# Attention plus feed-forward on one core: the first two rows' QKV interleaved by weight slice

## The chip, the cores and the metric

The kernel runs on one core of one Trainium2 chip. The metric is the device time of one execution in microseconds, as a median over runs. Below, PE is TensorE, DVE is VectorE, ACT is ScalarE, POOL is GpSimd and SP is SyncE, which here only issues DMAs.

## The reference

One transformer block on x of shape (1, 2048, 576), bf16, with no weights in the layer norm:

```python
xn = _layernorm(x, axis=-1)
return x + _A_ref(xn, A_wqkv, A_wo) + _B_ref(xn, B_w_gate, B_w_up, B_w_down)
```

`_A_ref` is attention with 32 heads of 18: `qkv = xn @ wqkv` (576 to 1728), each position attends to 8 positions, itself and those 2, 4, ... 14 before it, with a softmax over the 8 logits, and the result goes through `wo`. `_B_ref` is `(silu(xn @ w_gate) * (xn @ w_up)) @ w_down` with 4608 hidden columns.

## The kernel before

**Tiling.** The 2048 positions are 16 "rows" of 128: position 16p + r lies in partition p of row r. Four rows make a token tile of 512. A row of x is normalised on DVE (two `bn_stats` of 288 columns, one `bn_aggr`, a square root on ACT, a reciprocal, `ln_apply` and a small pad copy), and turned, so that the 576 columns lie in partitions, in five blocks `kt` of 128 (the last holds the 64 remaining columns twice): `xnT[:, kt, row]`.

**Turning a row.** There are three ways. `transp_pe` makes five 128x128 matmuls against the identity. `transp_halves` makes ten 64-row matmuls into two PSUM banks, of which ACT empties one and DVE the other. `transp_dma` issues a DMA transpose on SP. Before, rows 0 and 1 take the first way, rows 2 to 4 the second (inside the QKV of the row before) and rows 5 to 15 the third.

**QKV (L267).** A row needs four column groups `g` of 432 columns, each in a PSUM bank of its own, accumulated over the blocks `kt`. The weights come as five slices, one for each `kt` (`load_w`; the fifth as two DMAs). Row 0 (`p_row0`) uses 128-row matmuls, 4 x 4, then four 64-row ones for the fifth block. The other rows (`p_row`) use 36 64-row matmuls, two at a time in the two halves of the array, first groups 0 and 2, then 1 and 3, and then the same with the halves swapped; the callback `between` puts the next row's turning after 24 of the 36.

**Evacuation.** `p_evac` copies a row's four banks on ACT: Q to `QO`, K and V to staging tiles. After rows 4, 8, 12 and 15, `halo` moves four staged rows to the K and V rings, one partition further on, and `store` writes whole groups to DRAM.

**Order.** The program is written out by hand: each engine runs its instructions in the order of the source, and waits where a tile isn't ready. All PSUM tiles come from one pool of 8 banks, taken in rotation; a bank is written again when its last tile has been emptied. Nearly all DMAs are issued on SP, in source order; row 0's second half and the first weight slice are issued on ACT. Before the first real work, `warm_pe` runs matmuls on zeros.

**After QKV.** For each token tile, nine chunks of the gate and up matmuls (`g_pair`, L522) with SiLU on ACT (`g_evac`), and then the down projection and `wo` (`d_half`, L551). DVE runs the attention meanwhile: `chain(tt)` queues its pieces, and `dve.take` and `dve.pump` emit them at fixed places of the source. The chain of the first tile starts during QKV, since its keys come through the rings. This part is not touched.

Of the kernel before, what the change touches and what calls it, by code (L numbers as in the profile page):

```python
# [17 lines left out]
P = 128  # L18
# [52 lines left out]
def kernel(  # L71
# [70 lines left out]
    def load_x(eng, j, rows=slice(0, P)):  # L142
        eng.dma_start(xc_b[0][rows, j, :], x_v[rows, j, :])  # L143

    def load_w(eng, kt):
        if kt < 4:
            eng.dma_start(wqkv[:, kt, :], A_wqkv[kt * P:(kt + 1) * P, :])  # L147
        else:
            for i in range(2):
                eng.dma_start(wqkvr[64 * i:64 * i + 64, :], A_wqkv[4 * P:D, 2 * G * i:2 * G * (i + 1)])  # L150

    load_x(nc.sync, 0, slice(0, 64))
    load_x(nc.scalar, 0, slice(64, 128))
    load_w(nc.scalar, 0)
    make_identity(nc, ident[:])
    load_w(nc.sync, 1)
    load_x(nc.sync, 1)
    for kt in range(2, KT):
        load_w(nc.sync, kt)
    load_x(nc.sync, 2)  # L160
    load_x(nc.sync, 3)
    for c in range(1, 4):
        nc.sync.dma_start(xc_b[c], x_v[:, 4 * c:4 * c + 4, :])
# [4 lines left out]
    def warm_pe(n):  # L168
        for i in range(n):
            nc.tensor.matmul(wp[:], wz[:, 0:P], wz[:, 0:512], start=True, stop=True)  # L170
# [18 lines left out]
    def new_ps(name):  # L189
        return ps.tile([P, 512], f32, name=name, tag="ps")  # L190
# [4 lines left out]
    def ln_open(c):  # L195
        mv = lns.tile([P, 4, 2], f32, name="mv")
        rstd = lns.tile([P, 4], f32, name="rstd")
        ln[c] = (xc_b[c], xn_b[c % 2], mv, rstd)

    def ln_stats(r, n=1):  # L200
        c, j = divmod(r, 4)
        xc, xn, mv, rstd = ln[c]
        for i in range(j, j + n):
            stats = lns.tile([P, 2, 6], f32, name="stats")
            for k in range(2):
                nc.vector.bn_stats(stats[:, k, :], xc[:, i, k * HALF:(k + 1) * HALF])  # L206
            nc.vector.bn_aggr(mv[:, i, :], stats[:].rearrange("p c s -> p (c s)"))

    def ln_sqrt(r, n=1):
        c, j = divmod(r, 4)  # L210
        xc, xn, mv, rstd = ln[c]
        nc.scalar.activation(rstd[:, j:j + n], mv[:, j:j + n, 1], ACT.Sqrt, bias=eps_t[:], scale=1.0)  # L212

    def ln_recip(r, n=1):
        c, j = divmod(r, 4)
        rstd = ln[c][3]
        nc.vector.reciprocal(rstd[:, j:j + n], rstd[:, j:j + n])
# [9 lines left out]
    def transp_pe(r, kts, pt):  # L227
        c, j = divmod(r, 4)
        xn = ln[c][1]
        for i, kt in enumerate(kts):  # L230
            nc.tensor.transpose(pt[:, i * P:(i + 1) * P], xn[:, j, kt * P:(kt + 1) * P], ident[:])

    def copy_pt(eng, r, kts, pt):
        eng(xnT[:, kts[0]:kts[-1] + 1, r * P:(r + 1) * P],
            pt[:, 0:len(kts) * P].rearrange("p (k t) -> p k t", t=P))
# [4 lines left out]
    def transp_halves(r):  # L240


        c, j = divmod(r, 4)
        xn = ln[c][1]
        pt = [new_ps("pt") for half in range(2)]
        for kt in range(KT):
            for half in range(2):
                rows = slice(64 * half, 64 * half + 64)
                nc.tensor.matmul(pt[half][:, kt * 64:(kt + 1) * 64], xn[rows, j, kt * P:(kt + 1) * P],
                                 ident[rows, rows], start=True, stop=True)  # L250
        for half, eng in enumerate((nc.scalar.copy, nc.vector.tensor_copy)):
            lo = r * P + 64 * half
            eng(xnT[:, :, lo:lo + 64], pt[half][:, 0:KT * 64].rearrange("p (k t) -> p k t", t=64))
# [11 lines left out]
    def p_mm(t, g, kt, half, r, start, stop):  # L265
        rows = slice(0, P) if half is None else slice(64 * half, 64 * half + 64)
        return nc.tensor.matmul(t[g][:, 0:G], xnT[rows, kt, r * P:(r + 1) * P], w_at(g, kt, rows),  # L267
                                start=start, stop=stop)

    def p_row0(between):  # L270
        t = [new_ps("qkv_ps") for g in range(NG)]
        for kt in range(4):
            for g in range(NG):
                p_mm(t, g, kt, None, 0, kt == 0, False)
            if kt == 2:
                between()
        for i in range(2):
            for half in range(2):
                p_mm(t, i + 2 * half, 4, half, 0, False, True)
        return t  # L280

    def fence_after(mm):
        f = nc.gpsimd.engine_nop()
# [6 lines left out]
    def p_row(r, between=None):  # L290


        t = [None] * NG
        fence = {}
        for swap in range(2):
            for i in range(2):
                kts = (0, 1, 2, 3) if swap else (0, 4, 1, 2, 3)
                for kt in kts:
                    for half in range(2):
                        g = i + 2 * (half ^ swap)  # L300
                        if t[g] is None:
                            t[g] = new_ps("qkv_ps")
                        mm = p_mm(t, g, kt, half, r, swap == 0 and kt == 0, swap == 1 and kt == 3)
                        if swap == 0 and kt == 3 and half == 1:
                            fence[i] = fence_after(mm)
                        if swap and kt == 0 and half == 0:
                            fence_before(mm, fence[i])
                    if swap and i == 0 and kt == 1 and between is not None:
                        between()
        return t  # L310

    def p_evac(r, t, between=None):
        c, j = divmod(r, 4)
        ks, vs = stage[2 * c % 4], stage[(2 * c + 1) % 4]
        vdst = vs[:, j, :].rearrange("p (d h) -> p d h", h=H)

        def v_copy(lo, n, src):
            nc.scalar.copy(vdst[:, :, lo:lo + n], src.rearrange("p (h d) -> p d h", d=DH))  # L318

        nc.scalar.copy(QO[:, r, 0:G], t[0][:, 0:G])  # L320
        if between is not None:
            between()
        nc.scalar.copy(ks[:, j, HALF:D], t[2][:, 0:HALF])
        v_copy(0, 8, t[2][:, HALF:G])
        nc.scalar.copy(QO[:, r, G:D], t[1][:, 0:D - G])
        nc.scalar.copy(ks[:, j, 0:HALF], t[1][:, D - G:G])
        v_copy(8, 24, t[3][:, 0:G])

    def halo(m, c):
        ring = Kr if m == 1 else Vr  # L330
# [85 lines left out]
        dve.add(0.3, done)  # L416


    def pair_stats(r):
        if r % 4 == 0:  # L420
            ln_open(r // 4)
        ln_stats(r, 2)
        ln_sqrt(r, 2)

    def pair_apply(r):
        ln_recip(r, 2)
        for i in (r, r + 1):
            ln_apply(i)
            if i > 4:
                transp_dma(i)  # L430

    def first():
        pt = new_pt()
        transp_pe(1, range(KT), pt)
        copy_pt(nc.scalar.copy, 1, range(3), pt)
        copy_pt(nc.vector.tensor_copy, 1, range(3, KT), pt[:, 3 * P:])
        ln_stats(2)

    warm_pe(10)
    ln_open(0)  # L440
    ln_stats(0)
    ln_sqrt(0)
    ln_recip(0)
    ln_apply(0, 0, P)
    pa, pb = new_pt(), new_pt()
# [1 line left out]
    ln_apply(0, P, D)  # L447
    transp_pe(0, range(1, KT), pb)
    copy_pt(nc.scalar.copy, 0, (0,), pa)
    warm_pe(1)  # L450
    copy_pt(nc.scalar.copy, 0, (1, 2), pb)
    ln_stats(1)
    copy_pt(nc.vector.tensor_copy, 0, (3, 4), pb[:, 2 * P:])
    ln_sqrt(1)
    ln_recip(1)
    ln_apply(1)
    for r in range(R):
        if r == 0:
            t = p_row0(first)
        else:  # L460
            t = p_row(r, (lambda: transp_halves(r + 1)) if r <= 3 else None)
        if r == 1:
            ln_recip(3)
            ln_apply(3)
        if r == 0:
            p_evac(r, t, lambda: ln_sqrt(2))
            ln_recip(2)
            ln_apply(2)
            ln_stats(3)
            ln_sqrt(3)  # L470
        else:
            p_evac(r, t)
        if 2 <= r <= 7:
            pair_apply(2 * r)
        if 1 <= r <= 6:
            pair_stats(2 * r + 2)
        if r == 0:
            load_gu(0)
            load_wd(7)
        if r == 1:  # L480
            for ring in (Kr, Vr):
                nc.sync.dma_start(ring[0:1, 0:HALO, :], wz[0:1, :].unsqueeze(1).to_broadcast([1, HALO, D]))
        if r == 2:
            load_wd(8)
        if r in (4, 8, 12, R - 1):
            c = (r - 1) // 4 if r < R - 1 else 3
            for m in (1, 2):
                halo(m, c)
                if c in (1, 2):
                    store(m, c)  # L490
            if c == 3:
                store(1, c)
        if r == 9:
            load_gu(1)
        if r == 7:
            chain(0)
        if r in (7, 8, 12):
            dve.take(3 if r == 7 else 6)


    wo_order = list(range(DH))
# [134 lines left out]
```

## Time and profile before

| What | Value |
|---|---|
| median of 3 runs | 505.94 us (505.89 to 506.33) |
| the profiled execution's own time | 506.33 us |
| its span | 504.5 us |
| granted TensorE clock | 1.0 |
| PE busy | 498.9 us, 99% of the span |
| DVE busy | 327.6 us, 65% |
| ACT busy | 200.2 us, 40% |
| QKV matmuls (L267) | 560, 53.8 us busy |
| gate and up matmuls (L522) | 2592, 281.4 us busy |
| down and output matmuls (L551) | 2304 + 288, 152.1 + 28.6 us busy |

Times in the profile count from the start of the span. A timeline row gives an instruction's start and length, its engine and line, what it writes and reads, how many were merged into it, and in brackets the idle time ahead of it with what ended it. A matmul's length is longer than its distance to the next one, since matmuls are pipelined. PE's share of busy time counts matmuls that lie beside each other once.

### The profile page before, as it was taken

The page shows a single profiled execution, that of the slowest core. Times are in us where ns is not written, and L with a number is a line of the kernel's source. Part 1 is how long each engine was busy: PE and PEld are TensorE (multiplying, and loading weights), DVE is VectorE, ACT ScalarE, POOL GpSimd, SP SyncE. Part 2 cuts the span into 40 slices and gives each one's busy share as a digit, 9 for nine tenths or more (in the row PEclk, how much of TensorE's full clock was granted, in tenths as well). Part 3 has the DMA queues.
Part 4 walks back from the last instruction along what each step waited for, and adds up shares of the span by engine and source line. Part 5 has one row for each costly group of instructions (what it writes and reads, how often), then busy time and mean ns, then how long its engine had stood idle before and what let it go on. Part 6 is the DMA issues. An engine that isn't in the chain of part 4 may idle for free.

```text
span 504.5 us, 13260 instructions
## 1 busy us (share of the span) xinstructions
PE 498.9 (99%) x5799; PEld 349.4 (69%) x5799; DVE 327.6 (65%) x475; ACT 200.2 (40%) x416; POOL 0.7 (0%) x6
## 2 busy tenths in 40 slices
PE   8999999999999999999999999999999999999997
PEld 3555544555799855555999755556999555557997
DVE  4985699798999688999898129995990222221001
ACT  2766566655400164555300354558000454553000
POOL 0000000000000000000000000000000000000000
PEclk9999999999999999999999999999999999999999
DMA  8998988878932037546631053555600236452100
GB/s 274 275 216 197 323 266 261 261 226 265 250 108 61 25 97 220 155 142 196 141 118 48 26 187 114 169 172 161 145 25 14 90 114 186 141 189 40 27 14 25
DMA packets 75811, 75.26 MB, mean 149 GB/s; under 512 B 21972, under 2 KB 71536, under 8 KB 75752
## 3 DMA queue, kind: packets, MB, share of 16 engines
q1 hardware_dynamic: 75384, 73.82, 50.8%
q8 instruction: 45, 0.74, 0.6%
q10 hardware_dynamic: 368, 0.59, 0.4%
q14 instruction: 14, 0.11, 0.1%
HBM read 58.76 MB, written 5.90 MB: 128 GB/s over the span
## 4 chain that ended last, share of the span: by engine, by line
PE 95%; ACT 2%; DMA 1%; SPq 1%; DVE 1%; issue 1%; ACTq 0%
PE g_ps L522 54%; PE d_ps L551 31%; PE qkv_ps L267 9%; DMA wd<-in_A_x_dram 1%; ACT uc L534 1%; SPq L147 0%; DVE stats L206 0%; ACT L533 0%; ACT L392 0%; SPq L150 0%; ACT sg L533 0%; SPq L143 0%; ACT rstd L212 0%; ACT PP L392 0%; DVE wd L222 0%
## 5 line engine op out<-in xcount | busy, mean ns | idle before, releaser
L522 PE MATMUL g_ps<-xnT,gu 64*128 64x512 bf16 x2592 | 281.4, 376 | 0.0
L522 PEld LDWEIGHTS <-gu 64*128 64x128 bf16 x2592 | 160.0, 94 | 120.0 <-DMA gu<-in_B_w_up_dram 0.5
L551 PE MATMUL d_ps<-wd,hT 64*128 64x288 bf16 x2304 | 152.1, 283 | 0.0
L533 ACT ACTIVATE sg<-g_ps 128x512 bf16<-128x512 f32 x144 | 87.3, 606 | 157.2 <-PE g_ps L522 157.1
L551 PEld LDWEIGHTS <-hT 64*128 64x128 bf16 x2304 | 144.3, 94 | 0.5
L535 DVE TENSOR_TENSOR hT<-sg,uc 128x512 bf16<-128x512 bf16 x144 | 60.1, 419 | 93.8 <-ACT uc L534 93.8
L534 ACT CAST uc<-g_ps 128x512 bf16<-128x512 f32 x144 | 85.2, 592 | 0.0
L372 DVE TENSOR_REDUCE PP<-PP 128x64 f32<-128x1152 bf16 x64 | 84.9, 1346 | 0.4
L267 PE MATMUL qkv_ps<-hT,xnT 64*128 64x432 bf16 (+1 forms) x560 | 53.8, 343 | 0.8 <-DMA hT<-in_A_wqkv_dram 0.6
L367 DVE TENSOR_TENSOR PP<-QO,Kr 128x2304 bf16<-128x2304 bf16 (+1 forms) x35 | 43.5, 1250 | 11.0 <-DMA Kr<-hT 10.7
L563 DVE TENSOR_TENSOR ot<-d_ps,xr 128x288 bf16<-128x288 f32 x30 | 12.3, 451 | 51.0 <-PE d_ps L551 51.0
L267 PEld LDWEIGHTS <-xnT 64*128 64x128 bf16 (+1 forms) x560 | 27.7, 94 | 25.5 <-issue 1.4
L399 DVE TENSOR_TENSOR PP<-Vr,A 128x2304 bf16<-128x2304 bf16 (+1 forms) x35 | 43.3, 1250 | 0.4
L404 DVE TENSOR_TENSOR PP<-PP 128x2304 bf16<-128x2304 bf16 x24 | 32.5, 1354 | 0.3
L551 PE MATMUL d_ps<-wo,xnT 64*128 64x288 bf16 x288 | 28.6, 283 | 0.0
L533 ACT ACT_TABLE_LOAD x5 | 6.4, 1283 | 47.2 <-PE g_ps L522 47.2
L551 PEld LDWEIGHTS <-xnT 64*128 64x128 bf16 x288 | 20.8, 94 | 0.0
L392 ACT ACTIVATE PP<-PP 128x1024 f32<-128x1024 f32 x4 | 4.2, 1057 | 31.2 <-DVE PP L388 31.2
L566 ACT CAST ot<-d_ps 128x288 bf16<-128x288 f32 x1 | 0.4, 399 | 38.7 <-PE d_ps L551 38.7
L206 DVE BATCH_NORM_STATS2 stats<-wd 128x6 f32<-128x288 bf16 x32 | 12.7, 440 | 3.7 <-DMA wd<-in_A_x_dram 3.6
L318 ACT CAST hT<-qkv_ps 128x144 bf16<-128x144 f32 (+1 forms) x32 | 13.9, 435 | 2.5 <-DMA kv_d<-hT 2.5
L320 ACT CAST QO<-qkv_ps 128x432 bf16<-128x432 f32 x16 | 8.3, 518 | 8.4 <-PE qkv_ps L267 8.4
(40 smaller groups left out, 98.0 us busy)
## 6 DMA issues: line engine op xcount, KB each, us to landing
gu<-in_B_w_gate_dram SPq DMA_DIRECT2D x36, 512.0 KB, 4.0
gu<-in_B_w_up_dram SPq DMA_DIRECT2D x36, 512.0 KB, 5.4
wd<-in_B_w_down_dram SPq DMA_DIRECT2D x9, 576.0 KB, 5.9
kv_d<-hT SPq DMA_DIRECT2D x6, 576.0 KB, 5.4
gu<-in_B_w_gate_dram SPq DMA_DIRECT2D x36, 64.0 KB, 5.0
gu<-in_B_w_up_dram SPq DMA_DIRECT2D x36, 64.0 KB, 4.7
xr<-in_A_x_dram SPq DMA_DIRECT2D x4, 576.0 KB, 5.5
out_dram<-ot SPq DMA_DIRECT2D x15, 144.0 KB, 1.8
```

The source lines that it names most:

```text
L206: nc.vector.bn_stats(stats[:, k, :], xc[:, i, k * HALF:(k + 1) * HALF])
L267: return nc.tensor.matmul(t[g][:, 0:G], xnT[rows, kt, r * P:(r + 1) * P], w_at(g, kt, rows), start=start, stop=stop)
L318: nc.scalar.copy(vdst[:, :, lo:lo + n], src.rearrange("p (h d) -> p d h", d=DH))
L367: nc.vector.tensor_tensor(prod[:, a:b], QO[:, RT * tt + a:RT * tt + b, :], Kr[:, s:s + b - a, :], op=ALU.mult)
L372: nc.vector.tensor_reduce(L[:, w, rs], prod[:, rs].rearrange("p r (h d) -> p r h d", d=DH), axis=AX.X, op=ALU.add)
L399: nc.vector.tensor_tensor(dst[:, a:b], Vr[:, s:s + b - a, :].rearrange("p r (d h) -> p r d h", h=H), A[:, w, a:b].unsqueeze(2).to_broadcas ...
L404: nc.vector.tensor_tensor(dst, acc, pv, op=ALU.add)
L522: mm = nc.tensor.matmul(ring_ps[j][b][:], gu[rows, slot, k, fc], xnT[rows, kt, tok], start=(swap == 0 and kt == 0), stop=(swap == 1 and kt ...
L533: nc.scalar.activation(sg[:], t[0][:], ACT.Silu)
L534: nc.scalar.copy(uc[:], t[1][:])
L535: nc.vector.tensor_tensor(hT[:, ch * FC + j, :], sg[:], uc[:], op=ALU.mult)
L551: mm = nc.tensor.matmul(t[sub][h][:, 0:HALF], a[rows], w[rows, h * HALF:(h + 1) * HALF], start=(swap == 0 and n == 0), stop=(swap == 1 and ...
```

## The change

- x rows 0 and 1 are loaded first, each half on SP's queue and half on ACT's. All weight slices are then issued on SP; x row 2 goes ahead of the fourth slice (before: behind the fifth).
- Rows 0 and 1 share the stage: row 0's blocks 0 and 1, the turning of row 1, row 0's block 2, row 1's blocks 0 to 2 for groups 0, 2 and 1, row 0's block 3 and last block, row 1's block 3 and last block for groups 0 and 2, the turning of row 2 (by `transp_pe`), and row 1's group 3. Row 1 uses 128-row matmuls as row 0 does. Three of row 1's banks are open beside row 0's four.
- Row 0's groups 2 and 3 are emptied by DVE, not ACT. The warm-up matmul between row 0's transposes and its QKV is gone.
- DVE's work is in another order: half of row 1's statistics lies between row 0's square root and reciprocal. The statistics of rows 4 and 5 follow row 3's copy in row 2 (before: in row 1), and their square root is inside row 2's evacuation.
- Rows 5 and 6 are turned by TensorE too, within the rows before them. Rows 7 to 15 stay with the DMA. Row 7's transpose is issued after the halos of rows 0 to 3, those of rows 14 and 15 after the halos of rows 4 to 7.
- The first nine attention pieces are emitted after row 8 (before: three after row 7, six after row 8).

```diff
-    load_x(nc.sync, 0, slice(0, 64))
-    load_x(nc.scalar, 0, slice(64, 128))
-    load_w(nc.scalar, 0)
+    for j in range(2):
+        load_x(nc.sync, j, slice(0, 64))
+        load_x(nc.scalar, j, slice(64, 128))
     make_identity(nc, ident[:])
-    load_w(nc.sync, 1)
-    load_x(nc.sync, 1)
-    for kt in range(2, KT):
+    for kt in range(3):
         load_w(nc.sync, kt)
     load_x(nc.sync, 2)
+    for kt in range(3, KT):
+        load_w(nc.sync, kt)
     load_x(nc.sync, 3)
...
-    def p_row0(between):
...
+    def p_full(t, r, kts, gs):
+        for kt in kts:
+            for g in gs:
+                p_mm(t, g, kt, None, r, kt == 0, False)
+
+    def p_pair(t, r, i):
+        for half in range(2):
+            p_mm(t, i + 2 * half, 4, half, r, False, True)
...
-    def p_evac(r, t, between=None):
+    def p_evac(r, t, parts=(0, 2, 1, 3), copy=None, between=None):
...
+        for g in parts:
+            if g == 0:
+                copy(QO[:, r, 0:G], t[0][:, 0:G])
+            elif g == 2:
+                copy(ks[:, j, HALF:D], t[2][:, 0:HALF])
+                v_copy(0, 8, t[2][:, HALF:G])
+                if between is not None:
+                    between()
+            elif g == 1:
+                copy(QO[:, r, G:D], t[1][:, 0:D - G])
+                copy(ks[:, j, 0:HALF], t[1][:, D - G:G])
+            else:
+                v_copy(8, 24, t[3][:, 0:G])
...
+    def pair_apply(r, by_pe):
         ln_recip(r, 2)
         for i in (r, r + 1):
             ln_apply(i)
-            if i > 4:
+            if i > by_pe:
                 transp_dma(i)
...
+    def turn(r, na):
         pt = new_pt()
-        transp_pe(1, range(KT), pt)
-        copy_pt(nc.scalar.copy, 1, range(3), pt)
-        copy_pt(nc.vector.tensor_copy, 1, range(3, KT), pt[:, 3 * P:])
-        ln_stats(2)
+        transp_pe(r, range(KT), pt)
+        copy_pt(nc.scalar.copy, r, range(na), pt)
+        copy_pt(nc.vector.tensor_copy, r, range(na, KT), pt[:, na * P:])
...
     ln_sqrt(0)
+    half1 = ln_half(1, None, 0)
     ln_recip(0)
...
-    warm_pe(1)
     copy_pt(nc.scalar.copy, 0, (1, 2), pb)
-    ln_stats(1)
+    ln_half(1, half1, 1)
...
+    t0 = {g: new_ps("qkv_ps") for g in (0, 2, 1, 3)}
+    p_full(t0, 0, range(2), t0)
+    turn(1, 3)
+    p_full(t0, 0, (2,), t0)
+    t1 = {g: new_ps("qkv_ps") for g in (0, 2, 1)}
+    p_full(t1, 1, range(3), (0, 2, 1))
+    p_full(t0, 0, (3,), t0)
+    for i in range(2):
+        p_pair(t0, 0, i)
+    ln_stats(2)
+    ln_sqrt(2)
+    ln_recip(2)
+    ln_apply(2)
+    p_evac(0, t0, (0, 1))
+    p_evac(0, t0, (2, 3), nc.vector.tensor_copy)
+    p_full(t1, 1, (3,), (0, 2, 1))
+    p_pair(t1, 1, 0)
+    turn(2, 3)
+    t1[3] = new_ps("qkv_ps")
+    p_full(t1, 1, range(4), (3,))
+    p_pair(t1, 1, 1)
+    ln_stats(3)
+    load_gu(0)
+    load_wd(7)
...
+    p_evac(1, t1, between=lambda: ln_sqrt(3))
+    ln_recip(3)
+    ln_apply(3)
+
+    BY_PE = 6
+    for r in range(2, R):
+        t = p_row(r, (lambda: transp_halves(r + 1)) if r < BY_PE else None)
+        if r == 2:
+            ln_stats(4, 2)
+            p_evac(r, t, between=lambda: ln_sqrt(4, 2))
+            pair_apply(4, BY_PE)
+            load_wd(8)
+        elif r == 3:
+            p_evac(r, t)
+            ln_stats(6, 2)
+            ln_sqrt(6, 2)
+        elif r == 5:
+            ln_stats(9)
+            p_evac(r, t, between=lambda: ln_sqrt(8, 2))
+            pair_apply(8, BY_PE)
+            ln_stats(10, 2)
+            ln_sqrt(10, 2)
         else:
             p_evac(r, t)
...
         if r in (4, 8, 12, R - 1):
             c = (r - 1) // 4 if r < R - 1 else 3
             for m in (1, 2):
                 halo(m, c)
...
+        if r == 4:
+            pair_apply(6, BY_PE)
+            ln_stats(8)
+        if r in (6, 7):
+            pair_apply(2 * r - 2, BY_PE)
+            ln_stats(2 * r, 2)
+            ln_sqrt(2 * r, 2)
+        if r == 8:
+            pair_apply(14, BY_PE)
         if r == 9:
             load_gu(1)
-        if r == 7:
+        if r == 8:
             chain(0)
-        if r in (7, 8, 12):
-            dve.take(3 if r == 7 else 6)
+        if r in (8, 12):
+            dve.take(9 if r == 8 else 6)
```

More of the change, by code (lines that the diff above doesn't have):

```diff
@@ L200, in ln_stats, with ln_half @@
     def ln_stats(r, n=1):
+        for i in range(r, r + n):
+            stats = ln_half(i, None, 0)
+            ln_half(i, stats, 1)
+    def ln_half(r, stats, k):
         c, j = divmod(r, 4)
         xc, xn, mv, rstd = ln[c]
-        for i in range(j, j + n):
+        if k == 0:
             stats = lns.tile([P, 2, 6], f32, name="stats")
-            for k in range(2):
-                nc.vector.bn_stats(stats[:, k, :], xc[:, i, k * HALF:(k + 1) * HALF])
-            nc.vector.bn_aggr(mv[:, i, :], stats[:].rearrange("p c s -> p (c s)"))
+        nc.vector.bn_stats(stats[:, k, :], xc[:, j, k * HALF:(k + 1) * HALF])
+        if k == 1:
+            nc.vector.bn_aggr(mv[:, j, :], stats[:].rearrange("p c s -> p (c s)"))
+        return stats
     def ln_sqrt(r, n=1):
@@ L268, in p_mm @@
                                 start=start, stop=stop)
-    def p_row0(between):
[L271 to L280, printed above, removed]
+    def p_full(t, r, kts, gs):
[5 more added lines that the diff above has]
+            p_mm(t, i + 2 * half, 4, half, r, False, True)
     def fence_after(mm):
@@ L310, in p_row @@
         return t
-    def p_evac(r, t, between=None):
+    def p_evac(r, t, parts=(0, 2, 1, 3), copy=None, between=None):
         c, j = divmod(r, 4)
+        copy = copy or nc.scalar.copy
         ks, vs = stage[2 * c % 4], stage[(2 * c + 1) % 4]
@@ L317, in v_copy @@
         def v_copy(lo, n, src):
[L318 to L327, printed above, removed]
+            copy(vdst[:, :, lo:lo + n], src.rearrange("p (h d) -> p d h", d=DH))
+        for g in parts:
[11 more added lines that the diff above has]
+                v_copy(8, 24, t[3][:, 0:G])
     def halo(m, c):
@@ L416, in chain @@
         dve.add(0.3, done)
[L419 to L425, printed above, removed]
+    def pair_apply(r, by_pe):
         ln_recip(r, 2)
@@ L428, in pair_apply @@
             ln_apply(i)
-            if i > 4:
+            if i > by_pe:
                 transp_dma(i)
-    def first():
+    def turn(r, na):
         pt = new_pt()
-        transp_pe(1, range(KT), pt)
-        copy_pt(nc.scalar.copy, 1, range(3), pt)
-        copy_pt(nc.vector.tensor_copy, 1, range(3, KT), pt[:, 3 * P:])
-        ln_stats(2)
+        transp_pe(r, range(KT), pt)
+        copy_pt(nc.scalar.copy, r, range(na), pt)
+        copy_pt(nc.vector.tensor_copy, r, range(na, KT), pt[:, na * P:])
     warm_pe(10)
-    ln_open(0)
+    for c in range(RT):
+        ln_open(c)
     ln_stats(0)
     ln_sqrt(0)
+    half1 = ln_half(1, None, 0)
     ln_recip(0)
@@ L456 @@
     ln_apply(1)
[L457 to L470, printed above, removed]
+    t0 = {g: new_ps("qkv_ps") for g in (0, 2, 1, 3)}
[22 more added lines that the diff above has]
+    load_wd(7)
+    for ring in (Kr, Vr):
+        nc.sync.dma_start(ring[0:1, 0:HALO, :], wz[0:1, :].unsqueeze(1).to_broadcast([1, HALO, D]))
+    p_evac(1, t1, between=lambda: ln_sqrt(3))
[19 more added lines that the diff above has]
+            ln_sqrt(10, 2)
         else:
             p_evac(r, t)
[L473 to L484, printed above, removed]
         if r in (4, 8, 12, R - 1):
```

## The prediction

> **What bounds the kernel now.** I read the page's chain first: what released what, followed back from the end.
>
> ```profile
> PE 95%; ACT 2%; DMA 1%; SPq 1%; DVE 1%; issue 1%; ACTq 0%
> ```
>
> TensorE ends the run, so the change is worth what it does to TensorE's stream, nothing else. TensorE's waits over the whole span come second: four, all in the first 16 us, of which these two lie in QKV.
>
> ```profile
> PE qkv_ps L267 <- DMA hT<-in_A_wqkv_dram: 0.6, 1, 0.6
> PE qkv_ps L267 <- ACT xnT L253: 0.2, 1, 0.2
> ```
>
> Third, TensorE's timeline there (start, length, count, wait before). A length includes the matmuls' own latency, so I work with starts.
>
> ```profile
> 6.02 0.91 PE L231 MATMUL pt<-ident,wd 128*128 128x128 bf16 x5 [0.32 <-DVE wd L222]
> 6.72 0.61 PE L170 MATMUL warm_ps<-ot 128*128 128x512 bf16 x1
> 7.15 2.41 PE L267 MATMUL qkv_ps<-hT,xnT 128*128 128x432 bf16 x12
> 9.40 0.44 PE L231 MATMUL pt<-ident,wd 128*128 128x128 bf16 x5
> 10.45 3.55 PE L267 MATMUL qkv_ps<-hT,xnT 128*128 128x432 bf16 x32 [0.61 <-DMA hT<-in_A_wqkv_dram]
> 13.84 0.31 PE L249 MATMUL pt<-ident,wd 64*128 64x64 bf16 x10
> 13.98 1.26 PE L267 MATMUL qkv_ps<-hT,xnT 64*128 64x432 bf16 x12
> 15.43 2.36 PE L267 MATMUL qkv_ps<-hT,xnT 64*128 64x432 bf16 x24 [0.19 <-ACT xnT L253]
> 17.63 0.31 PE L249 MATMUL pt<-ident,wd 64*128 64x64 bf16 x10
> ```
>
> Prices from it: a full 128x432 matmul follows the last by 0.183 us; a 64-row pair takes the same (24 matmuls, 15.43 to 17.63, 2.20). A row of 36 half matmuls is 3.29; 16 full ones and 4 halves are 2.93 + 0.38 = 3.31, so 128-row matmuls are no dearer. Five full transposes take 0.28, ten half ones 0.15 (13.84 to 13.98). Row 2 starts at 15.43. The gate stage (L522) starts at 61.83, so nine rows earlier row 7 starts at 32.26, and rows 4 to 6 put row 4 at 22.40.
>
> **Up to row 2.** DVE gets one half of row 1's statistics between row 0's square root and reciprocal. It starts after the aggregate (5.08) and lasts 0.41, so the reciprocal moves from 5.45 to 5.52: +0.07, if x row 1 has landed by 5.1. x row 0 landed 2.3 and 3.2 after its issue; the same from issues at 1.35 gives 3.7 to 4.6. The removed warm matmul held the stream from 6.72 to 7.15: -0.43. First QKV matmul: 6.80.
>
> From there: row 0's first two slices, 8 x 0.183, to 8.26. Row 1's normalised half is ready when recip and apply, moved up by 0.4 (half its statistics are done) less 0.07, end at 8.4, so 0.16 of waiting; transposes 0.28, to 8.70; row 0's third slice 0.73, to 9.43; nine matmuls of row 1, 1.64, to 11.07; row 0's fourth slice and pairs, 1.11, to 12.18; three matmuls and a pair of row 1, 0.74, to 12.92; row 2's five transposes 0.28; row 1's last column group, 0.92. Row 2 starts at 14.12, 1.31 earlier. Row 0's four banks leave by ACT and DVE together (0.41+0.17+0.29 and 0.35+0.2+0.5) before 13.5, under row 1's matmuls; without that cover row 1's fourth bank would wait 0.4.
>
> Whether the slices come in time: the third landed at 8.6 before (issued 2.71, 5.9 to landing) and is wanted at 8.70; the last at 11.25 (4.35, 6.9), wanted at 11.80. The same bytes lie ahead of the third; x row 2 (144 KB at some 360 GB/s, 0.4 us) now lies ahead of the last. The first slice moves from ACT's queue (issued 1.33) to third place on SP's, behind two issues of 0.58 and 0.43 or more: some 0.5 us later. Bounds: 0 (bytes decide), and 0.9 (both 0.5 and 0.4 fall on the last slices). Below zero is out, as no slice moves ahead. I take 0.2, nearer to the bytes, since the DMA engines' share is 0.8 to 0.9 in every microsecond from 2 to 19. **Row 2: 14.3.** The Trainium skill (DMA: Bandwidth & Descriptors, Issuing engines are not separate DMA queues) says that DMAs of several issuing engines share the same 16 DMA engines and that a second queue saves only issue time; by it this term is 0 to 0.5, and the sum would stand between -0.2 and +0.3 of mine.
>
> **Rows 3 and 4.** Row 3's transposes come 2.2 into row 2, where its pad copy is just ready: 0.1. Row 4's come at R2 + 3.43 + 2.2 = R2 + 5.63, R2 being row 2's start. But DVE now starts the statistics of rows 4 and 5 only after row 3's copy (before: at 15.85, 0.4 into row 2). The copy starts 0.38 after the transposes and holds DVE 0.41: R2 + 2.99. What follows is measured on the next pair:
>
> ```profile
> 19.72 0.81 DVE L206 BATCH_NORM_STATS2 stats<-wd 128x6 f32<-128x288 bf16 x2
> 20.57 0.21 DVE L207 BATCH_NORM_AGGREGATE mv<-stats 128x2 f32<-128x12 f32 x1
> 20.69 0.77 DVE L206 BATCH_NORM_STATS2 stats<-wd 128x6 f32<-128x288 bf16 x2
> 21.49 0.21 DVE L207 BATCH_NORM_AGGREGATE mv<-stats 128x2 f32<-128x12 f32 x1
> ...
> 22.27 0.43 DVE L222 TENSOR_SCALAR wd<-wd,mv,rstd 128x576 bf16<-128x576 bf16 x1
> ```
>
> 19.72 to 22.70 is 2.98, so row 4 is normalised at R2 + 5.97. The square root is queued on ACT inside row 2's evacuation: behind it wait the evacuations of two banks. It starts at R2 + 2.99 + 2.02 and with 0.20 + 0.17 + 0.29 + 0.57 after it the last bank is empty at R2 + 6.24. In the rotation of eight banks that is one of the two that row 4's transposes write. They start 0.65 late; the bounds are 0.4 (data only) and 0.8. **Row 4: 14.3 + 6.86 + 0.1 + 0.65 = 21.9, 0.5 earlier than before.**
>
> **Rows 5 to 7.** Two more rows turned by TensorE: +0.30. Row 7 could start at 21.9 + 2 x 3.43 + 3.29 = 32.05, 0.2 earlier. But it is the first that a DMA turns, and its DMA now stands on SP behind the six halo DMAs of rows 0 to 3, which wait for row 3's evacuation. Before, the order on SP was rows 6 to 9, then these:
>
> ```profile
> 29.21 0.61 SPq L335 DMA_DIRECT2D Kr<-hT  x1
> ...
> 33.00 0.88 SPq L338 DMA_DIRECT2D Vr<-hT  x1
> 33.99 9.48 SPq L257 DMA_TRANSPOSE xnT<-wd  x6
> ```
>
> From the first halo to the transpose behind them: 4.78. Row 3's K is evacuated about 1.05 after row 4 starts, so row 7's transpose is issued 5.85 after it, at 27.75. Row 7 wants it 10.15 after row 4's start, so 4.3 are left for landing. DMA transposes landed in 2.6 to 5.5; the nearest row is the first behind the halos, row 10's:
>
> ```profile
> xnT<-wd SPq DMA_TRANSPOSE x1, 5.5
> ```
>
> The next one took 4.3. So the wait lies between 0 and 1.2. I take 4.8, hence 0.5, between the two, because row 10's transpose had five more queued right behind it and row 7's has none. **Row 7: 32.55 against 32.26, +0.3.** Rows 8 and 9 are issued about 30 and 31.5, wanted at 35.8 and 39.1: hidden.
>
> **At no cost.** The pools opened early issue nothing. The first attention pieces (DVE) move behind row 8, but DVE waited 5.85 and 4.88 us for K's ring in this stage, so 3.4 us fit. Rows 14 and 15 are now turned behind the halos of rows 4 to 7, landing by 53 against a start of row 14 near 55. The gate and down weights keep their place behind the x loads. After QKV every instruction is the same.
>
> The profiled run took 506.33 with a span of 504.5, so 1.83 lie around it; the median is 505.94, 0.39 below that run. I add the difference of +0.3 to the median: **506.2**.
>
> **Rivals.** (1) *The transpose is in time.* Landing in 4.3 and slices on time: -0.2 - 0.2, so 505.5; if row 4's stall is also gone, 504.8. For it: 2.6 us landings away from halos. Against: 5.5 behind them. The Trainium skill (DMA: Bandwidth & Descriptors, Anatomy of one DMA) gives a fixed cost of 2.0 us and bytes at 436 GB/s, fitted for GpSimd's path; an estimate by that page lands row 7 at 2.4 after issue, in time, with 505.7. The trace does not agree behind halos, with 5.5. A gain is capped in any case: at 87.85 ACT's exponential starts only 0.5 after DVE has its input (87.32), and DVE had worked without a pause since 60.77. What is gained beyond 0.5 may be waited away there.
>
> (2) *Slower: the slices are late.* One queue carries all weights, TensorE wants the third at 8.70 and the last at 11.80, and the margins are 0.1 and 0.55. From there each us late is a us of wait, and every later step hangs on row 2's start. At 9.6 and 12.7 row 2 starts near 15.0 and the time is 506.2 - 0.2 + 0.9 = 506.9; with row 7's full 1.2 it is 507.6. For it: landings of 5.9 to 7.2 us, and the last slices' 0.61 wait in the profile. Against: before and after, the same bytes come first.
>
> (3) *Row 7 waits the whole 1.2*, slices as in the sum: 506.9, the upper end of the forecast.
>
> **Numbers.** Forecast with (3) 0.47, rival 1 0.23, rival 2 0.30. 0.2% is 1.0 us, about what a measurement of this kernel tells from no change. Faster by more than that needs rival 1 without row 4's stall: 0.14. Slower by more needs rival 2 beyond 0.9 (0.24) or the forecast with row 7's 1.2 and another 0.2 (0.16): 0.40. The rest, 0.46, is within. Range: 505.0, most of rival 1, to 507.8, rival 2 with row 7's wait.
>
> **What would show it.** First QKV matmul at 6.8; row 2 at 14.1 to 14.5, with a wait on weights no longer than 0.4; before row 4's transposes a TensorE wait of 0.4 to 0.8 on DVE or on ACT's evacuation; before row 7 a wait on the DMA of xnT; the gate stage at 62.1. It is wrong if row 4's transposes wait for nothing, if row 2 starts after 15, or if a wait appears behind row 7 that the trace of before does not have.

## The result, and the profile after

The changed kernel takes 507.32 us (median of 17 runs, 506.73 to 508.55), the kernel before 506.12 beside it (17 runs): ratio 1.0026, 95% interval 1.0019 to 1.0033. It is slower by 1.2 us, where +0.3 was forecast. The profiled execution took 506.78 us with a span of 504.9; before, 506.33 and 504.5.

The first line of the chain of waits of the kernel after; TensorE still ends the run, ACT's share has gone, DMA's is larger:

```profile
PE 96%; DMA 2%; DVE 1%; SPq 0%; issue 0%; ACT 0%
```

Its waits lie in QKV again, and TensorE's timeline of the kernel after shows where:

```profile
6.46 1.63 PE L273 MATMUL qkv_ps<-hT,xnT 128*128 128x432 bf16 x8
...
8.88 4.76 PE L273 MATMUL qkv_ps<-hT,xnT 128*128 128x432 bf16 x26 [0.43 <-DMA hT<-in_A_wqkv_dram]
13.57 0.45 PE L237 MATMUL pt<-ident,wd 128*128 128x128 bf16 x5
13.86 3.37 PE L273 MATMUL qkv_ps<-hT,xnT 128*128 128x432 bf16 x30
17.07 0.31 PE L255 MATMUL pt<-ident,wd 64*128 64x64 bf16 x10
...
20.89 0.42 PE L255 MATMUL pt<-ident,wd 64*128 64x64 bf16 x10 [0.22 <-DVE wd L228]
...
28.00 4.54 PE L273 MATMUL qkv_ps<-hT,xnT 64*128 64x432 bf16 x48
33.04 29.74 PE L273 MATMUL qkv_ps<-hT,xnT 64*128 64x432 bf16 x324 [0.49 <-DMA xnT<-wd]
62.61 3.62 PE L557 MATMUL g_ps<-xnT,gu 64*128 64x512 bf16 x32
```

The weights' wait is smaller than before (0.43 for 0.61); those of row 4's transposes on DVE and of row 7 on its transpose are new. Two marks are enough to read all runs below. Row 2 starts 24 matmuls (2.20 us) before row 3's transposes: 17.07 - 2.20 gives 14.87 here (14.88 by the single records), 15.43 before. The gate stage starts at 62.61, 61.83 before. So the first rows won 0.55, and rows 2 to 6 lost 1.34. The 48 matmuls at 28.00 are 12 of row 5 and row 6's 36: row 7 could have begun at 28.00 + 48 x 0.0915 = 32.39 and began at 33.04, its 324 matmuls of nine rows running on to the gate stage without a pause.

From the gate stage on nearly every kernel here takes the same: execution time less gate start is 444.2 in the profile after, 444.1 in the first experiment (the same kernel again), 444.0 in the kernel before when it was profiled again, and 443.9 to 444.2 in twelve of the fourteen profiles. There are two exceptions. The first profile of before has 444.5: it lost 0.4 at 93.3 to gate weights. The first kernel with rows 4 and 7 mended together has 444.6: at 136.55, behind the gate stage, TensorE waited for a DMA transpose of the attention's output. The first profile of before therefore flattered the change: 506.78 is 1.16 above the second one (505.62), about what these medians say.

### The profile page after: what moved, and what is told of

Same layout as the page of the kernel before. It is cut to its first block, busy times and chain, and to the rows that moved or that the text cites. A ratio compares the mean times of both kernels' runs of the same rounds, so it can differ in the third digit from the quotient of the medians.

```text
span 504.9 us, 13257 instructions
## 1 busy us (share of the span) xinstructions
PE 498.9 (99%) x5797; PEld 283.6 (56%) x5797; DVE 329.7 (65%) x480; ACT 200.6 (40%) x415; POOL 0.7 (0%) x6
## 4 chain that ended last, share of the span: by engine, by line
PE 96%; DMA 2%; DVE 1%; SPq 0%; issue 0%; ACT 0%
PE g_ps L557 55%; PE d_ps L586 32%; PE qkv_ps L273 9%; DMA hT<-in_A_wqkv_dram 1%; DMA xnT<-wd 1%; DVE stats L210 0%; SPq L143 0%; SPq L147 0%; PE pt L255 0%; DVE xnT L259 0%; DVE ot L601 0%; DVE wd L228 0%; DVE mv L212 0%; PE pt L237 0%; ACT rstd L218 0%
## 5 line engine op out<-in xcount | busy, mean ns | idle before, releaser
L557 PEld LDWEIGHTS <-gu 64*128 64x128 bf16 x2592 | 126.6, 94 | 152.5
L586 PE MATMUL d_ps<-wd,hT 64*128 64x288 bf16 x2304 | 146.3, 283 | 0.0
L586 PEld LDWEIGHTS <-hT 64*128 64x128 bf16 x2304 | 112.4, 94 | 29.5
L568 ACT ACT_TABLE_LOAD x5 | 6.4, 1283 | 47.2 <-PE g_ps L557 47.2
L586 PE MATMUL d_ps<-wo,xnT 64*128 64x288 bf16 x288 | 22.9, 283 | 0.0
L586 PEld LDWEIGHTS <-xnT 64*128 64x128 bf16 x288 | 14.1, 94 | 3.6
```

The source lines that it names most:

```text
L557: mm = nc.tensor.matmul(ring_ps[j][b][:], gu[rows, slot, k, fc], xnT[rows, kt, tok], start=(swap == 0 and kt == 0), stop=(swap == 1 and kt ...
L568: nc.scalar.activation(sg[:], t[0][:], ACT.Silu)
L586: mm = nc.tensor.matmul(t[sub][h][:, 0:HALF], a[rows], w[rows, h * HALF:(h + 1) * HALF], start=(swap == 0 and n == 0), stop=(swap == 1 and ...
```

## Experiments

Three theories. **A**: the loss lies inside QKV, in waits that the change makes itself (row 4's normalisation, row 7's transpose behind the halos, the slices and the matmul forms). **B**: the gate stage, started at another time, meets late weights or ACT's exponential. **C**: how x and the weights are ordered on the queues makes the first rows late, and by how much differs from run to run.

The marks and times of all runs (us; the median of before was measured beside it, on the same chip):

| Kernel | row 2 | gate | gate less row 2 | median | before | ratio, 95% |
|---|---|---|---|---|---|---|
| before_again | 15.18 | 61.58 | 46.40 | 505.77 | 505.55 | 1.0001 (0.9992 to 1.0010) |
| after_again | 17.70 | 65.45 | 47.74 | 507.49 | 505.34 | 1.0048 (1.0033 to 1.0063) |
| row7_before_v_halo | 14.54 | 61.62 | 47.07 | 506.74 | 505.34 | 1.0030 (1.0016 to 1.0044) |
| row4_alone | 14.92 | 62.54 | 47.62 | 507.64 | 505.34 | 1.0040 (1.0028 to 1.0052) |
| slice0_on_act | 14.70 | 62.62 | 47.91 | 506.80 | 505.34 | 1.0027 (1.0017 to 1.0036) |
| slices_first | 15.91 | 63.66 | 47.75 | 507.43 | 505.55 | 1.0028 (1.0005 to 1.0050) |
| mended_one_queue_less | 14.53 | 61.84 | 47.32 | 506.54 | 505.55 | 1.0021 (1.0011 to 1.0032) |
| mended_slices_first | 16.16 | 63.48 | 47.32 | 507.00 | 505.55 | 1.0022 (1.0010 to 1.0033) |
| row7_and_pairs_together | 14.02 | 61.15 | 47.13 | 506.05 | 506.13 | 1.0002 (0.9991 to 1.0012) |
| x1_ahead_on_sp | 14.03 | 61.10 | 47.07 | 505.98 | 506.13 | 0.9998 (0.9985 to 1.0012) |
| all_mended | 14.65 | 62.43 | 47.78 | 506.86 | 506.13 | 1.0018 (1.0005 to 1.0032) |
| row4_row7_x1_pairs | 14.87 | 61.56 | 46.69 | 504.96 | 505.51 | 0.9988 (0.9975 to 1.0001) |

### The two kernels again

Both are unchanged.

> The changed kernel once more, for a second profile. Its first profile has a span 0.4 us over that of before, while the medians lie 1.2 us apart, so one profile may not be typical. Theory A (the loss is three waits within QKV: the third weight slice, row 4's turning, row 7's DMA transpose): the same three waits, of 0.2 to 0.9, 0.4 to 0.6 and 0.4 to 1.0 us, and a time of 506.7 to 507.6. Theory B (the loss is in the gate stage, where the weights of a chunk come late): the gate stage's first 9 chunks take over 70.2 us, against 69.9 in the first profile of the changed kernel and 70.3 in that of before.

The profile fell on an execution of 509.58 us. TensorE's timeline of this second run of the kernel after:

```profile
6.17 0.90 PE L273 MATMUL qkv_ps<-hT,xnT 128*128 128x432 bf16 x4
9.11 1.60 PE L273 MATMUL qkv_ps<-hT,xnT 128*128 128x432 bf16 x4 [2.04 <-DMA hT<-in_A_wqkv_dram]
10.51 0.74 PE L237 MATMUL pt<-ident,wd 128*128 128x128 bf16 x5
```

Slice 1 landed late, TensorE stood for 2.04 us, and the four matmuls after it took 1.40 to the transposes, where four take 0.73. The same run by windows (PE, weight loads, DVE, ACT, POOL, granted clock, DMA share, GB/s):

```profile
8.00:10.00 2.00, 0.89 (x3) 0.40 (x3) 0.00 (x0) 0.00 (x0) 0.00 (x0) 0.78 1.03 370
10.00:12.00 2.00, 2.00 (x10) 1.12 (x9) 0.21 (x2) 0.48 (x1) 0.00 (x0) 0.50 1.09 277
```

The granted clock fell to half, and was back at 1.00 from 14 on (0.86 from 12 to 14): some 3.4 us at half, from 9.1 to 12.5. Row 2 starts 2.83 later than in the first profile, the gate stage 2.83, the execution ends 2.80 later: what is late at row 2 stays late, and row 2 to gate is 47.7 in both. Theory B has nothing to explain, C has one case.

The medians of the same two kernels lie 2.15 apart here (interval 1.0033 to 1.0063), where they lay 1.2 apart at first. A profile catches one execution, and it lies up to 1.1 from the median of its kernel, here 2.1. Medians are therefore compared only with the before beside them, and what a row costs is read from the marks.

> The kernel of before once more, for a second profile. Its runs scatter from 504.7 to 507.2, with the first profile at 506.33 in the upper part. Theory C (the change costs more than its profiles show, since the runs scatter by when the weight slices land): this profile, if it is of a run near 505.3, shows the fourth slice landing earlier than 10.4 or no wait at the fifth gate chunk (0.4 in the first profile), and row 2 starting near 15.0 or before. Theory A: row 2 at 15.2 to 15.5 again, and the same QKV to within 0.3.

TensorE's timeline of the kernel before, second run, has row 3's transposes 0.25 earlier than the first:

```profile
17.38 0.31 PE L249 MATMUL pt<-ident,wd 64*128 64x64 bf16 x10
```

Row 2 to gate is 46.40, so the change costs 1.34 there in each pair of profiles. The first nine gate chunks take 69.93 here, as in the kernel after. Theory B falls: of all profiles only the first of before lost anything in the gate stage.

### Row 7's transpose ahead of the V halos

```diff
             pair_apply(8, BY_PE)
+            halo(2, 0)
...
-            for m in (1, 2):
+            for m in (1, 2) if c else (1,):
```

> The three V halo DMAs of rows 0 to 3 are issued behind the transposes of rows 8 and 9, so row 7's transpose has only K's three ahead of it on SP. Theory A: row 7's transpose is issued at about 26.6 instead of 28.4, lands before 31, TensorE's wait of 0.65 us ahead of row 7 is gone, and the time falls by 0.5 to 0.7, to 506.5 to 506.9. Theory B: the wait goes, but the gate stage waits for its weights instead, and the time falls by under 0.3.

In the kernel after, SP's queue has the six halo DMAs first:

```profile
23.26 0.58 SPq L344 DMA_DIRECT2D Kr<-hT  x1
...
28.43 8.68 SPq L263 DMA_TRANSPOSE xnT<-wd  x5
```

and the chain of waits of that kernel gives the landing, so at 33.00 row 7's x is there:

```profile
28.43 4.57 DMA xnT<-wd
```

SP's queue with the V halos behind:

```profile
26.29 6.83 SPq L263 DMA_TRANSPOSE xnT<-wd  x3
```

and TensorE's timeline of the same kernel:

```profile
27.67 34.11 PE L273 MATMUL qkv_ps<-hT,xnT 64*128 64x432 bf16 x372
```

These 372 matmuls, 12 of row 5 and ten rows of 36, run without a pause to the gate stage at 61.62. Row 4's wait is untouched (0.22 at 20.55). Row 2 to gate falls by 0.66: row 7's share of theory A, shown.

### Row 4 normalised alone, ahead of row 5

```diff
-            ln_stats(4, 2)
-            p_evac(r, t, between=lambda: ln_sqrt(4, 2))
-            pair_apply(4, BY_PE)
+            ln_stats(4)
+            p_evac(r, t, between=lambda: ln_sqrt(4))
+            ln_recip(4)
+            ln_apply(4)
+            ln_stats(5)
+            ln_sqrt(5)
             load_wd(8)
         elif r == 3:
             p_evac(r, t)
+            ln_recip(5)
+            ln_apply(5)
```

> DVE takes the statistics, square root, reciprocal and apply of row 4 by themselves, and those of row 5 after them. Theory A: row 4 is normalised about 1.0 us earlier, its transposes (20.9 in the changed kernel, 0.38 late, and another 0.11 for a bank) start on time at 20.5, and the time falls by 0.4 to 0.5, unless row 7's wait takes it back: if that wait is set by row 3's evacuation, it moves with row 4 and the gain stays; if the landing is fixed in time, the wait grows to about 1.1 and the gain is 0. Theory B: under 0.2.

TensorE's timeline with row 4 alone:

```profile
20.54 0.31 PE L255 MATMUL pt<-ident,wd 64*128 64x64 bf16 x10
...
32.97 12.22 PE L273 MATMUL qkv_ps<-hT,xnT 64*128 64x432 bf16 x132 [0.82 <-DMA xnT<-wd]
```

and ACT's:

```profile
21.16 0.29 ACT L218 ACTIVATE rstd<-mv,eps_t 128x1 f32<-128x1 f32 x1 [0.99 <-DVE mv L212]
```

Row 4's stall is gone, and TensorE reaches row 7 earlier by just that much, only to wait for a transpose that comes no earlier: its issue hangs on row 3's evacuation, and row 5's square root now holds ACT for 0.99 ahead of it. The gain of one mend fell into the other wait (row 2 to gate 47.62, not 47.2).

### The first weight slice back on ACT's queue

```diff
+    load_w(nc.scalar, 0)
     make_identity(nc, ident[:])
-    for kt in range(3):
+    for kt in range(1, 3):
```

> The first weight slice is issued on ACT's queue behind the two x halves, as it was before (there behind one), the rest on SP's as in the change. If the third slice is late because one queue issues all (the 0.5 us that the prediction left open): it lands 0.3 to 0.5 earlier, TensorE's wait of 0.43 at 8.88 shrinks to 0.1 or less, row 2 starts 0.3 earlier and the time falls by about 0.3. If the bytes set it: the wait stays within 0.1 of 0.43 and the time is the same within 0.2.

The profile shows little: row 2 at 14.70, and the third slice's matmuls at 8.79 instead of 8.88, behind waits of 0.33 and 0.16 for the first two slices. The median is 0.7 below that of the kernel after, measured beside it; the two intervals overlap a little, so this is a hint that the loads cost more in other executions than in the profiled one.

### Row 1's x behind slice 1

```diff
-    for j in range(2):
-        load_x(nc.sync, j, slice(0, 64))
-        load_x(nc.scalar, j, slice(64, 128))
+    load_x(nc.sync, 0, slice(0, 64))
+    load_x(nc.scalar, 0, slice(64, 128))
+    load_w(nc.scalar, 0)
     make_identity(nc, ident[:])
-    for kt in range(3):
-        load_w(nc.sync, kt)
+    load_w(nc.sync, 1)
+    load_x(nc.sync, 1)
+    load_w(nc.sync, 2)
...
-    half1 = ln_half(1, None, 0)
...
-    ln_half(1, half1, 1)
+    ln_stats(1)
```

> The change with the loads in about the order of before: SP has x row 0's first half, slice 1, x row 1, slice 2, x row 2, slices 3 and 4; ACT has x row 0's second half and slice 0. Row 1's statistics are whole again, behind row 0's apply. Theory C: the order of loads costs the change its time: slices 1 and 2 land before they are wanted (7.0 and 8.6), no run has the wait of 2.0 us with a slow clock that the second profile of the change shows, the highest time is under 508.3, and the median falls by 0.7 to 1.2 to 506.3 to 506.8. Theory A: row 7's fixed landing takes what is gained before it, and the median falls by under 0.4.

TensorE's timeline:

```profile
7.41 1.62 PE L274 MATMUL qkv_ps<-hT,xnT 128*128 128x432 bf16 x8 [0.79 <-DMA hT<-in_A_wqkv_dram]
9.68 0.45 PE L238 MATMUL pt<-ident,wd 128*128 128x128 bf16 x5 [0.65 <-DVE wd L229]
```

A miss for theory C: TensorE now waits for slice 0 and then for row 1, and row 2 starts at 15.91. By the trace's packets SP's slice 1 went ahead of ACT's slice 0 (last packets 4.75 and 6.94). To load x row 1 behind a slice, with x row 2 still ahead of the last slices, is no cure.

### Rows 4 and 7 mended together

Mended_one_queue_less has slice 0 on ACT, row 4 alone, row 5's square root inside row 3's evacuation, and K's halos ahead of row 7's transpose, V's behind. Mended_slices_first has the loads of the experiment above instead. What is new against the two single mends:

```diff
         elif r == 3:
-            p_evac(r, t)
+            p_evac(r, t, between=lambda: ln_sqrt(5))
+            ln_recip(5)
+            ln_apply(5)
```

> The change with three edits: V's halo of rows 0 to 3 behind the transposes of rows 8 and 9, the first slice on ACT's queue, and row 4 normalised by itself, with row 5's square root inside row 3's evacuation, so that ACT is not held up. Theory A: no wait ahead of rows 4 and 7, and the gains add: 0.65 + 0.45 and what the slice brings (0.7 in the median): 505.7 to 506.2, against 507.5. If a later wait takes the place of row 7's, 506.5 or more.

> The change with the loads and statistics of slices_first, and with V's halo moved and row 4 by itself. Theories A and C together: no wait ahead of rows 4 and 7, slices in time, row 2 near 14.5 to 14.8, row 7 near 31.7, time 505.0 to 505.6, so level with before or faster by up to 0.3. If the slices still come late: 505.8 or more.

TensorE's timeline of the first of them:

```profile
25.55 2.36 PE L274 MATMUL qkv_ps<-hT,xnT 64*128 64x432 bf16 x24 [0.57 <-ACT xnT L260]
```

The waits of rows 4 and 7 are gone, and a new one stands at row 5: ACT copies its half of row 5's columns behind the square root of rows 6 and 7, which waits for DVE. The second kernel has the same wait (0.57 at 27.18) and row 2 at 16.16. Both give 47.32 from row 2 to gate, so row 2 to gate does not depend on the loads, as theory A has it.

### Matmuls of one form together, and x row 1 whole on SP

Both have row 7's mend. The first moves row 1's fourth block ahead of row 0's last one; the second instead loads x row 1 on SP and slice 0 on ACT.

```diff
+    p_full(t1, 1, (3,), (0, 2, 1))
     for i in range(2):
         p_pair(t0, 0, i)
...
-    p_full(t1, 1, (3,), (0, 2, 1))
     p_pair(t1, 1, 0)
```

> The kernel row7_before_v_halo with one more edit: row 1's fourth block (three 128-row matmuls) comes ahead of row 0's 64-row pairs, so that the pairs of both rows are adjacent and two changes between 128-row and 64-row matmuls fall away. If each change costs 0.09 us (starts 0.275 apart in place of 0.183, six times in the changed kernel's profile): the stretch from row 0's third block to row 2 takes 0.18 less (5.82 instead of 6.00), if no slice is late in it. If the 0.09 is a wait for something else: 5.95 or more. The time cannot tell 0.18.

> The kernel row7_before_v_halo with x row 1 whole on SP's queue, and the first slice on ACT's queue directly behind x row 0's half, where it was before; the other slices follow on SP. If x row 1's place ahead of the first slice makes all slices late (their last packets came 0.7 to 0.9 later in the change than before): slice 0 ends near 4.9 (5.6 in the change), slice 2 near 7.6 (8.0), there is no wait on slices over 0.2, and the median is 505.7 to 506.3. If the slices scatter whatever the order: 506.5 or more, as slices_first.

TensorE's timeline with the forms together:

```profile
8.30 4.46 PE L273 MATMUL qkv_ps<-hT,xnT 128*128 128x432 bf16 x26
12.70 0.45 PE L237 MATMUL pt<-ident,wd 128*128 128x128 bf16 x5
```

and with x row 1 on SP, the forms as in the change:

```profile
8.10 4.70 PE L274 MATMUL qkv_ps<-hT,xnT 128*128 128x432 bf16 x26
12.72 0.45 PE L238 MATMUL pt<-ident,wd 128*128 128x128 bf16 x5
```

The same 26 matmuls, 20 full ones and three pairs: 23 x 0.183 = 4.21. To the transposes behind them they take 4.40 with two changes between 128-row and 64-row form, and 4.62 with four. A change of form costs 0.10 us: in the single records a matmul behind one starts 0.275 to 0.286 after its neighbour in place of 0.183, in the kernel before too (11.28).

Both kernels reach the time of before. Not all of that is theirs: in the profiles they start row 2 only 0.5 earlier than row7_before_v_halo, whose median lay 1.4 above the before beside it. Nor did slice 0 end near 4.9 in x1_ahead_on_sp, as its expectation had it, but at 5.56; slice 2 ended at 7.2. Why these medians are so good stays open.

### All rows singly

On top of the mends, rows 4, 5, 6, 8 and 9 are normalised one by one, with their square roots inside evacuations (rows 6 and 7 share one, row 9's stands behind row 5's evacuation), x row 1 on SP, slice 0 on ACT, and the forms together.

```diff
-            ln_stats(6, 2)
-            ln_sqrt(6, 2)
+            ln_stats(6)
+        elif r == 4:
+            ln_stats(7)
+            p_evac(r, t, between=lambda: ln_sqrt(6, 2))
         elif r == 5:
+            ln_stats(8)
+            p_evac(r, t, between=lambda: ln_sqrt(8))
...
```

> x1_ahead_on_sp and the pairs together, with rows 4, 5 and 6 normalised one row at a time, each square root inside the evacuation of a row whose statistics are ready, and V's halo behind the transposes of rows 8 and 9. Theory A with the scatter of slices: no wait between row 2 and the gate stage over 0.2, row 2 at 14.3 to 14.6, the gate stage at 61.0 to 61.3 (before: 61.6 and 61.8), time 0.2 to 0.5 below before in runs with slices in time, the median 505.0 to 505.8. If a wait moves on to another row again, the gate stage starts at 61.6 or later.

ACT's timeline:

```profile
37.99 0.30 ACT L219 ACTIVATE rstd<-mv,eps_t 128x2 f32<-128x2 f32 x1 [1.57 <-DVE mv L213]
```

A miss: the wait moved on to later rows. The square root of one pair waits 1.57 here, that of the pair before 2.81. Each such square root ahead of a row's evacuation waits for DVE and holds that row's banks; TensorE waits about 0.3 for banks at 35.6, 39.2 and 42.9. Row 2 to gate is 47.78, as bad as unmended. Several rows change at once here, and which of them makes DVE late is not separated.

### Rows 4 and 7, x row 1 and the forms

Row4_alone, row7_before_v_halo, x1_ahead_on_sp and the forms together, nothing else.

> x1_ahead_on_sp (V's halo behind row 9's transpose, x row 1 whole on SP, the first slice on ACT's queue) with the pairs together and row 4 by itself as in row4_alone, where no wait but row 7's was left. Theory A: the wait of 0.4 to 0.5 ahead of row 4's transposes is gone and, with row 7's gone too, the gain stays; two changes of matmul form save another 0.2. From row 2's start to the gate stage 46.7 (47.1 in x1_ahead_on_sp, 46.4 in before), the gate stage at 60.5 to 60.8, the profiled time 504.5 to 504.9, the median 505.3 to 505.8 against 506.0 of x1_ahead_on_sp, 0.3 to 0.6 below before measured beside it. If the wait moves on, as in all_mended: 47.1 or more from row 2, and the median at or above before.

TensorE's timeline:

```profile
17.07 0.36 PE L256 MATMUL pt<-ident,wd 64*128 64x64 bf16 x10
...
27.61 34.11 PE L274 MATMUL qkv_ps<-hT,xnT 64*128 64x432 bf16 x372
61.56 4.70 PE L564 MATMUL g_ps<-xnT,gu 64*128 64x512 bf16 x42
```

No wait behind row 2. Row 2 to gate is 46.69, which is 46.40 and the 0.30 of two more rows turned by TensorE. That it fits within 0.01 is partly chance: before loses 0.09 at 22.40, and here row 3's transposes and the matmuls behind row 4's take 0.05 longer than usual, each. The median is 0.55 below that of before beside it, the best of all, though the interval (0.9975 to 1.0001) just reaches no change.

## Why the prediction was right, and where it was off

The time lies in the forecast's range, but at +1.2, where the forecast was +0.3. The account behind row 2 held; the account up to row 2 was short, and the range holds the time because it reached as far as rival 2. By its steps:

**Rows 3 to 7 and the gate stage.** Forecast from row 2 to the gate stage: 62.1 - 14.3 = 47.8. Measured: 47.7, in both profiles. The terms, one by one:

- *Row 4's transposes 0.65 late, the data at R2 + 5.97 and the last bank at R2 + 6.24.* With R2 at 14.88 that is 20.85 and 21.12. The mechanism is right and the size a little high: the stall is 0.49. DVE's timeline of the kernel after has row 3's copy, behind it the statistics of both rows, and the normalised row 4 at 20.83:

```profile
17.45 0.49 DVE L259 CAST xnT<-pt 128x320 bf16<-128x320 f32 x1 [0.41 <-PE pt L255]
...
20.40 0.43 DVE L228 TENSOR_SCALAR wd<-wd,mv,rstd 128x576 bf16<-128x576 bf16 x1
```

  and ACT's has the square root waiting, and the bank empty at 21.05:

```profile
19.87 0.29 ACT L218 ACTIVATE rstd<-mv,eps_t 128x2 f32<-128x2 f32 x1 [1.05 <-DVE mv L212]
...
20.52 0.53 ACT L322 CAST hT<-qkv_ps 128x432 bf16<-128x432 f32 x1
```

  TensorE starts the transposes at 20.89 instead of 20.50 and takes 0.25 over them instead of 0.15: 0.39 for the data, 0.10 for the bank.
- *Row 7's wait 0.5, from a landing of 4.8 behind the halos, bounds 0 to 1.2.* The landing was 4.57 and the wait 0.65 (33.04 less 32.39). Two errors nearly cancel in it: the transpose was issued 6.19 after row 4's start (28.43 less 22.24), not 5.85, and landed 0.23 sooner than taken. Without the V halos ahead the wait vanishes. The estimate in rival 1 from the fixed cost in the Trainium skill (DMA: Bandwidth & Descriptors, Anatomy of one DMA), 2.4, was far off behind halos, where even with the V halos moved behind it the landing was 4.1; it is near the 2.6 of the transposes of rows 8 to 11.
- *Two more rows turned by TensorE, +0.30.* Right: in the last experiment it is what is left, to within 0.1.

The three make 1.44, 0.1 more than the measured 1.34, because the kernel before lost 0.1 at row 4 too (22.40, where 15.43 + 2 x 3.43 is 22.29).

**Row 2 at 14.3.** Here the step failed: it was 14.88. "16 full ones and 4 halves are 3.31, so 128-row matmuls are no dearer" is a sum of durations, without the change from one form to the other. Each costs 0.10, the new order has five up to row 2's start and the old one had one. From the third slice's first matmul to row 2 the prediction had 14.12 - 8.70 = 5.42, and it took 14.88 - 8.88 = 6.00; five changes are 0.5 of the 0.58, and 0.09 more is at the fourth slice, which landed at 11.29: its first matmul starts at 11.34, 0.275 behind a neighbour of its own form. The Trainium skill (TensorEngine Tiling (Array Packing), Key Properties) says that changing the tiling mode drains TensorE. The trace agrees that each change costs, with 0.10 us; it does not show that a drain is the reason.

**The slices, 0.2.** In the profiled run that was about right. The third slice's matmuls began at 8.88 where 8.70 was forecast (it landed at 8.83, 0.2 later than the 8.63 of before), and the fourth slice cost the 0.09. By the last packets all five slices came 0.7 to 0.9 later than before (slice 2 at 8.04 against 7.34, slice 4 at 11.32 against 10.43), which is the upper bound, but TensorE wanted the late ones late enough. The first QKV matmul stood at 6.46 instead of 6.80, as x row 0 landed sooner; that gained nothing, since the third slice was waited for. The reading that the bytes decide rested on a DMA share of 0.8 to 0.9; by windows of 1 us it was 0.82 to 1.12.

**Rival 2** was the nearest by its number, row 2 near 15.0 and +0.9, but not by its mechanism in the profiled run, where the forms made row 2 late more than the slices. Its rule, that each us late is a us of wait, held in the second run of the kernel after (2.83 at row 2, 2.83 at the gate stage). Row 2 started at 17.70 there, so one sign of being wrong that the prediction named, a start after 15, did come, in one profile of two. If every execution takes 444.1 from the gate stage and 47.74 ahead of that, the median of 507.32 has row 2 at 15.5, an estimate; the same sum with 444.0 and 46.40 puts it at 15.7 for the median of before, 506.12. Both are later than in the profiles named first, 14.88 and 15.43, and the change wins some 0.2 up to row 2 and not 1.1. That the slices came later in most executions is argued from two profiles of each kernel and the medians, not shown; what makes the landings differ is open. Rival 1 did not come about. Its cap at ACT's exponential was not met: in x1_ahead_on_sp the gate stage starts 0.73 earlier than in the first profile of before, and 444.05 still follow.

**The sum.** Measured +1.2 against before: +1.34 from row 2 to the gate stage, and -0.1 by the median where the forecast had -1.1. Of the missing 1.0, the four extra changes of form are 0.4, shown; the other 0.6 I put down to the loads, which is argued, and no run here separates it. At 0.26% it lies just past the bound of 0.2%, where the prediction had put 0.40, against 0.46 for a time within it.

## What to carry to other kernels

A count of matmuls by their pitch is not a sum of their time when neighbours differ in form: price each change, and put matmuls of one form together. A stall that is taken away in a chain of rows can reappear at the next row whose square root, bank or transpose hangs on the same engine: read row by row which one is next, and mend those together. When an early load decides, one profile is one draw: two marks in the trace, one behind the loads and one where the steady part starts, separate what scatters from what the code costs.

## What the runs showed of the hardware

- A change between 128-row and 64-row form among 432-column matmuls cost 0.10 us each time (26 matmuls: 4.40 with two changes, 4.62 with four).
- In one execution a wait of 2.04 us for weights was followed by a granted TensorE clock of 0.50 for some 3.4 us. The Trainium skill (TensorE: Matmul & The Clock Gate, Part 1) puts the fall behind an idle window of about 3.4 us; the trace shows it after a shorter pause. A wait of 1.07 us for the first slice (mended_slices_first) was followed by none.
- A DMA transpose of one row landed 4.57 us after its issue with six halo DMAs ahead of it, and after 2.8 to 4.4 with three. The sooner it was issued behind the last halo, the longer it took: counted from the issue of that halo, the landing came after 5.9 (kernel after) and 6.5 (before, first transpose behind them) with six, and after 5.4 to 6.0 with three.
- Of two loads issued on SP and ACT within the first microseconds either can be first: slice 0 from ACT ended at 4.72 in the kernel before, ahead of slice 1, and at 6.94 in slices_first, behind it.
